# Experts 1 to 7 of a mixture make their first product by Strassen's algorithm

## The chip, the core and the metric

The kernel runs on one core of a Trainium2 chip. Five engines work side by side, each through its own instructions in order: TensorE (PE, matrix products into PSUM), VectorE (DVE), ScalarE (ACT), GpSimd (POOL, no access to PSUM, also issues indirect transfers) and SyncE (SP, issues the other transfers). They wait for each other by semaphores. The metric is the device time of one execution in microseconds, median of several. PSUM has eight banks of 512 float32 values per partition.

## The reference

`setup_inputs` gives q, k, v (4 batches, 8 heads, 768 positions, 64 values) and the weights of a mixture of 8 experts. Local and block-compressed attention makes x, 3072 rows of 512. Then every row goes to its two best experts:

```
logits = x @ w_gate;  noisy = logits + log1p(exp(x @ w_noise)) * noise
top2 = two largest of noisy;  top2_w = softmax over the two
for e in range(8):
    for k in range(2):
        mask = top2[:, k] == e
        h = np.maximum(x[mask] @ w1[e], 0.0)                     # 512 -> 1024
        out[mask] += top2_w[mask, k, None] * (h @ w2[e])         # 1024 -> 512
```

## The kernel before

Attention and gating fill the first 150 us or so; the change doesn't touch them. A table then says which rows each expert has. Space is made for 816 rows (`CAP`) per expert, in seven chunks: six of 128 and one of 48.

Every float32 operand is split into two float16 values, a high part (rounded) and a low part (the rest). A product is three products: high by high, low weight by high, high weight by low. ACT makes a high part by a copy, DVE the low part as operand minus high part.

For each expert:

- `x_gather` (POOL) fetches a chunk's rows of x, high and low side by side, into one of four buffers `xg`; `x_trans` (SP) transposes them by a transfer into `xte`, 8 blocks of 128 partitions (4 high, 4 low) by 816 rows.
- `w_load` (SP) fetches a quarter of a weight matrix, 512 KB, into one of four buffers `stg`; `w_split` makes its high part on ACT and its low part on DVE. Both weight matrices have two sets of buffers, one for odd experts and one for even ones.
- First product: for two halves of the rows (384 and 432 wide) and eight blocks f of 128 of the 1024 columns, `mm1` runs 12 matmuls into a bank `h` (four banks in turn). ACT writes `hth` = relu(h) in float16, DVE writes `htl` = max(h, 0) - hth.
- Second product: for each chunk, three passes of eight matmuls into a bank `pt` (two banks in turn): `hth` by `w2h`, `htl` by `w2h`, `hth` by `w2l`. Then DVE makes `y` = pt x gate + `prev`, where `prev` (three buffers) holds the rows of `out` as earlier experts left them, fetched by POOL; POOL writes y back to those rows.

What prepares expert e + 1 is issued in steps between the pieces of expert e: `ticks` is called after each block of the first product and each chunk of the second, and `next_loads` issues at each call one load and split, or one gather and transpose. So the order of each engine's instructions is the order of the program's text, and an engine that waits for one instruction holds up all that stand behind it in that order.

The last lines of the program, under `tc.If`, serve inputs where an expert has more than 816 rows; with these inputs they don't run.

Of the kernel before, what the change touches and what calls it, by code (L numbers as in the profile page):

```python
# [59 lines left out]
def attn_moe(ctx, tc, qt, kt, vt, wgn, noise, w1, w2, out):  # L60
# [565 lines left out]
    def w_lo(e, i):  # L626
        n, sc = ("w1", W1S) if i < 4 else ("w2", W2S)
        hi, lo = [WT[e][n + x][:, i % 4, :] for x in "hl"]
        nc.vector.scalar_tensor_tensor(lo, SG[e, i], sc, hi, op0=OP.mult, op1=OP.subtract)  # L629

# [112 lines left out]
    def mm2_high(e, c, hook=None, py=None):  # L743
        PY[c] = psum.tile([P, 512], F32, name="pt", bufs=2) if py is None else py
        mm2_pass(e, c, "w2h", HT[0], 0, PY[c])
        if hook:
            hook()
        mm2_pass(e, c, "w2h", HT[1], 1, PY[c])

    def mm2_low(e, c, pv):  # L750
# [4 lines left out]
        gw = (TL[:, e] if c == LAST else tb_of(e, c)).bitcast(F32)[:, 1:2]
        if pv is None:
            nc.vector.tensor_scalar(y, py[:, :d], gw, None, op0=OP.mult)
# [297 lines left out]
    late_k = k
    tick = [0]

    def ticks(e):
        if e == 1 and tick[0] + late_k < 18:
            next_loads(1, tick[0] + late_k)  # L1060
        else:
            next_loads(e + 1, tick[0] - (18 - late_k if e == 1 else 0))
        tick[0] += 1

    for e in range(1, E):
        tick[0] = 0
        pv = []
        for half in range(2):
            for f in range(FC):
                mm1(e, half, f)  # L1070
                ticks(e)
                if tick[0] > 13:
                    pv.append(prev_gather(e, len(pv)))
# [112 lines left out]
```

## Time and profile before

| | |
|---|---|
| median of 3 runs | 702.61 us |
| lowest, highest | 702.22, 704.16 us |
| span of the profiled execution | 701.2 us |
| mean granted clock of TensorE | 0.992 |
| busy in that span: PE, DVE, ACT, POOL | 668.8, 314.2, 236.4, 248.4 us |
| transfers | 125.90 MB, 180 GB/s on average |

The profile is of one execution; its own time outside the span isn't given, and the median lies 1.4 us above its span. In the lines of the profile, L690 is the matmul of the first product, L740 and L737 those of the second (six whole chunks, the last chunk), L700 and L701 the high and low part of h, L612 and L629 those of the weights, L757 and L759 y, L86 POOL's indirect transfers, L604 and L607 the loads of weights, L668 the transposes. L352, L512 and L622 lie in the attention and gating: L352 is a POOL subtraction of two operands, L512 and L622 are DVE instructions with two operands in SBUF. Idle time behind a group is time in which its engine had nothing running, with what ended it.

### The profile page before, as it was taken

Reading aid. Unit: us, or ns where it says so; the run is one execution under the profiler, and the core shown is the slowest. Engines: PE = TensorE matmul, PEld = TensorE weight load, DVE = VectorE, ACT = ScalarE, POOL = GpSimd, SP = SyncE. Lnnn points to the kernel's source line nnn. Section 1 sums busy time; section 2 is a strip of 40 time slices with the busy share of each in tenths; the row PEclk is TensorE's granted clock in tenths of the full one; section 3 lists DMA queues with packets and bytes.
Section 4 is the critical chain, followed back from the end, with each engine's and each line's share of the span. In section 5 each row is a group of like instructions: output and inputs, shape, how many; then the busy total and the mean of one; then the engine's idle time right before and its main releaser. Section 6 shows DMA issues by size and latency. Waiting matters only on the chain.

```text
span 701.2 us, 14039 instructions
## 1 busy us (share of the span) xinstructions
PE 668.8 (95%) x5568; PEld 386.3 (55%) x5568; DVE 314.2 (45%) x663; ACT 236.4 (34%) x538; POOL 248.4 (35%) x435
## 2 busy tenths in 40 slices
PE   7999889889999999999999999999999999999993
PEld 6677667665445544654465456545554555455442
DVE  5758898789443533253134314521442155122110
ACT  2879788842231430142024203400430043012100
POOL 3445344502605305432343234233414441530141
PEclk9999999999999999999999999999999999999997
DMA  9999998867885997494259617921994196320021
GB/s 285 303 281 332 275 318 271 240 178 285 213 195 157 195 218 200 138 264 168 87 124 218 200 68 184 306 67 69 178 231 151 64 211 186 103 61 16 28 80 35
DMA packets 100295, 125.90 MB, mean 180 GB/s; under 512 B 58985, under 2 KB 63857, under 8 KB 100220
## 3 DMA queue, kind: packets, MB, share of 16 engines
q1 hardware_dynamic: 88076, 88.64, 48.3%
q0 software_dynamic: 12144, 36.28, 17.6%
q8 instruction: 46, 0.75, 0.5%
q14 instruction: 29, 0.24, 0.1%
HBM read 87.57 MB, written 26.21 MB: 162 GB/s over the span
## 4 chain that ended last, share of the span: by engine, by line
PE 82%; DVE 7%; ACT 4%; DMA 3%; issue 1%; SPq 0%; POOL 0%; POOLq 0%; DVEq 0%
PE h L690 37%; PE pt L740 35%; PE pt L737 3%; ACT p L304 2%; PE pt L310 2%; DMA hth<-in_vt_dram 1%; PE s L290 1%; DMA q<-in_qt_dram 1%; PE o L323 1%; DVE rh L535 1%; DVE nm L297 1%; ACT pts L313 1%; DMA kb<-in_kt_dram 1%; PE pt L235 1%; DVE kmax L218 1%
## 5 line engine op out<-in xcount | busy, mean ns | idle before, releaser
L690 PE MATMUL h<-xte,w1h 128*128 128x432 f16 (+1 forms) x1024 | 199.4, 336 | 0.6 <-ACT xte L677 0.6
L700 ACT ACTIVATE hth<-h 128x432 f16<-128x432 f32 (+1 forms) x128 | 64.1, 508 | 301.1 <-PE h L690 289.2
L690 PEld LDWEIGHTS <-w1h 128*128 128x128 f16 x1024 | 99.5, 98 | 76.8 <-issue 2.0
L86 POOL DMA_INDIRECT out_dram<-y,tb x48 | 53.2, 1109 | 249.0 <-DVE y L759 219.3
L740 PEld LDWEIGHTS <-hth 128*128 128x128 f16 x768 | 75.0, 98 | 90.0 <-ACT hth L700 0.8
L701 DVE SCALAR_TENSOR_TENSOR htl<-h,hth 128x432 f16<-128x432 f32 (+1 forms) x128 | 73.3, 580 | 94.7 <-ACT hth L700 89.5
L690 PE MATMUL h<-xte,w1l 128*128 128x432 f16 (+1 forms) x512 | 109.3, 336 | 0.0
L759 DVE SCALAR_TENSOR_TENSOR y<-pt,tb,prev 128x512 f32<-128x512 f32 x42 | 31.5, 751 | 162.0 <-PE pt L740 157.6
L86 POOL DMA_INDIRECT xg<-xd,tb x56 | 60.8, 1085 | 92.7 <-DMA xte<-xg 55.5
L740 PE MATMUL pt<-w2h,hth 128*128 128x512 f16 x376 | 89.2, 379 | 0.0
L740 PE MATMUL pt<-w2h,htl 128*128 128x512 f16 x376 | 88.8, 379 | 0.0
L740 PE MATMUL pt<-w2l,hth 128*128 128x512 f16 x376 | 88.7, 379 | 0.0
L690 PEld LDWEIGHTS <-w1l 128*128 128x128 f16 x512 | 50.1, 98 | 38.0
L740 PEld LDWEIGHTS <-htl 128*128 128x128 f16 x384 | 37.6, 98 | 45.2
L304 ACT ACTIVATE p<-s,nm 128x118 f32<-128x118 f32 x192 | 53.3, 376 | 0.8
L629 DVE SCALAR_TENSOR_TENSOR w2l<-stg,w2h 128x1024 f16<-128x1024 f32 x32 | 38.8, 1222 | 26.0 <-ACT w2h L612 21.6
L612 ACT ACTIVATE w2h<-stg 128x1024 f16<-128x1024 f32 x32 | 33.7, 1053 | 49.9 <-DMA stg<-in_w_dram 49.8
L352 POOL TENSOR_TENSOR xr<-x,xr 128x512 f16<-128x512 f32 x22 | 25.4, 1156 | 63.0 <-ACT xr L345 35.2
L86 POOL DMA_INDIRECT prev<-out_dram,tb x42 | 42.6, 1015 | 10.8 <-issue 10.8
L629 DVE SCALAR_TENSOR_TENSOR w1l<-stg,w1h 128x1024 f16<-128x1024 f32 x28 | 34.3, 1225 | 25.7 <-ACT w1h L612 24.9
L612 ACT ACTIVATE w1h<-stg 128x1024 f16<-128x1024 f32 x28 | 29.4, 1051 | 15.0 <-DMA stg<-in_w_dram 14.8
L310 PE MATMUL pt<-ident,p 128*118 128x128 f32 x192 | 29.7, 286 | 1.6 <-ACT p L304 1.6
(166 smaller groups left out, 572.1 us busy)
## 6 DMA issues: line engine op xcount, KB each, us to landing
stg<-in_w_dram SPq DMA_DIRECT2D x64, 512.0 KB
hth<-in_vt_dram SPq DMA_DIRECT2D x8, 780.0 KB
vw<-in_vt_dram SPq DMA_DIRECT2D x32, 195.0 KB
q<-in_qt_dram SPq DMA_DIRECT2D x24, 256.0 KB
xd<-xr SPq DMA_DIRECT2D x24, 256.0 KB
out_dram<-xg SPq DMA_DIRECT2D x8, 768.0 KB
kb<-in_kt_dram SPq DMA_DIRECT2D x6, 768.0 KB
htl<-in_vt_dram SPq DMA_DIRECT2D x16, 195.0 KB
```

What stands on the lines that cost most here:

```text
L86: return nc.gpsimd.indirect_dma_start(**kw)
L304: nc.scalar.activation(PE_[t][:, a, hp, :], SC[t][:, a, hp, :], AF.Exp, bias=NM[t][:, 1, a, hp:hp + 1], scale=0.125)
L310: nc.tensor.transpose(pt[:NK, hp, :], PE_[t][:, a, hp, :], ident)
L352: engine.tensor_tensor(XR[t][:, DM:], X[t], XR[t][:, 0:DM], op=OP.subtract)
L612: nc.scalar.activation(WT[e][n + "h"][:, i % 4, :], SG[e, i], AF.Copy, scale=sc)
L629: nc.vector.scalar_tensor_tensor(lo, SG[e, i], sc, hi, op0=OP.mult, op1=OP.subtract)
L690: nc.tensor.matmul(ph[:, :n], w[wn][:, c, f * P:(f + 1) * P], x[:, xo + c, c0:c1], start=(k == 0), stop=(k == 11), skip_group_check=hook i ...
L700: nc.scalar.activation(hh[:, f, c0:c1], ph, AF.Relu)
L701: nc.vector.scalar_tensor_tensor(hl[:, f, c0:c1], ph, 0.0, hh[:, f, c0:c1], op0=OP.max, op1=OP.subtract)
L737: nc.tensor.matmul(py[64 * r:64 * r + 64, :HD], hx[:, f, c * P:c * P + 64], w[:, f, HD * r:HD * r + HD], start=first, stop=final, skip_gro ...
L740: nc.tensor.matmul(py, hx[:, f, c * P:c * P + P], w[:, f, :], start=first, stop=final, skip_group_check=True)
L759: nc.vector.scalar_tensor_tensor(y, py[:, :d], gw, pv[:, :d], op0=OP.mult, op1=OP.add)
```

## The change

For experts 1 to 7 the first product is cut into 2 by 2 blocks: the 512 values that are summed over into two halves, the 1024 columns into two halves, and the 816 rows into two halves of 408. Seven products of blocks take the place of eight, by the variant of Strassen's algorithm with shared sums:

```
w1 as blocks:  a.l a.r (upper half of the 512)   b.l b.r (lower half)
x as blocks x[half of the 512][half of the rows], low and high part joined
S1 = a.r + b.r     S2 = S1 - a.l      S3 = a.l - a.r     S4 = b.l - S2
T1 = x01 - x00     T3 = x11 - x01     T2 = T3 + x00      T4 = x10 - T2
P1 = a.l x00   P2 = b.l x10   P3 = S4 x11   P4 = b.r T4   P5 = S1 T1   P6 = S2 T2   P7 = S3 T3
u2 = P6 + P1       u3 = P6 + P7 + P1
left columns:  first rows a = P1 + P2     second rows c1 = P5 + P3 + u2
right columns: first and second rows c2 = P4 + u3 | P5 + u3
```

The sums and their places in the code stand in the diff. The sums S are made by POOL (`w1_sums`) and split by ACT and DVE (`w1_pair`); b.r of the loaded weight goes into its place, S4 takes the place of a.r. The differences of x are made by POOL (`t_diff`), the rest of the T by DVE, and split again by ACT (`t_hi`) and DVE (`t_lo`). `mm1_quad` makes the products of one block f of 128 columns in each half of the columns, four times per expert, in the order P1, P6, P5, P7, P4, P2, P3. P1 and P2 gather in a bank `o` of two; P6 and P7 in one bank `h`, P5 and P3 in a second, P4 in a third. P7 is added to the bank of P6, and u2 reads P6 from it in between, so P7 waits for u2.

The second weights have one set of buffers in place of two and are split during the first product of their own expert. Steps are now written into `plan`: 28 in the first product (after each of the seven products), 21 in the second (after the first and second pass and after y). Of a y there are two buffers in place of four. In expert 0, whose matmuls stay as they were, all that prepares expert 1 is issued in 13 steps, among them what was done in expert 1 before.

```diff
     def w_alloc(e):
+        w1_alloc(e)
+        w2_alloc(e)
+
+    def w1_alloc(e, sums=False):
         pool = late[0] if e % 2 else wpool
-        WT[e] = {n: pool.tile([P, 4, 1024], F16, name=f"{n}{e % 2}") for n in ("w1h", "w1l", "w2h", "w2l")}
+        WT[e] = {n: pool.tile([P, 4, 1024], F16, name=f"{n}{e % 2}") for n in ("w1h", "w1l")}
...
+    def w2_alloc(e):
+        for n in ("w2h", "w2l"):
+            WT[e][n] = wpool.tile([P, 4, 1024], F16, name=n)
...
+    def w1_sums(e, k):
+        a, b = SG[e, k], SG[e, k + 2]
+        s = WS_[e, k] = side_pool[0].tile([P, 4, HF], F32, name="ws")
+        nc.gpsimd.tensor_tensor(s[:, 0], a[:, HF:], b[:, HF:], op=OP.add)
+        nc.gpsimd.tensor_tensor(s[:, 2], a[:, :HF], a[:, HF:], op=OP.subtract)
+        nc.gpsimd.tensor_tensor(s[:, 1], s[:, 0], a[:, :HF], op=OP.subtract)
+        nc.gpsimd.tensor_tensor(s[:, 3], b[:, :HF], s[:, 1], op=OP.subtract)
+
+    def w1_pair(e, k, part):
...
+        if part == 0:
+            todo_ = [(hi[:, k, :HF], lo[:, k, :HF], SG[e, k][:, :HF]),
+                     (hi[:, k + 2], lo[:, k + 2], SG[e, k + 2])]
+        else:
+            s = WS_[e, k]
+            todo_ = [(w["sh"][:, :, k], w["sl"][:, :, k], s[:, 0:3]),
+                     (hi[:, k, HF:], lo[:, k, HF:], s[:, 3])]
+        for h, _, x in todo_:
+            nc.scalar.activation(h, x, AF.Copy, scale=W1S)
+        for h, l, x in todo_:
+            nc.vector.scalar_tensor_tensor(l, x, W1S, h, op0=OP.mult, op1=OP.subtract)
...
+    def t_diff(e, j, low):
+        i = (1, 1) if j == 3 else (0, 1)
+        o = (0, 1) if j == 3 else (0, 0)
+        nc.gpsimd.tensor_tensor(tt(e, (j, low)), xb(e, *i, low), xb(e, *o, low), op=OP.subtract)
...
+    def h_split(f, c0, c1, c, hook=None):
+        hh, hl = HT
+        nc.scalar.activation(hh[:, f, c0:c1], c, AF.Relu)
...
+        nc.vector.scalar_tensor_tensor(hl[:, f, c0:c1], c, 0.0, hh[:, f, c0:c1], op0=OP.max, op1=OP.subtract)
+
+    def mm1_quad(e, f, oa, tick):
...
+        a = oa[:, f % 2, :HC]
+        product(a, e, f, 1, True, False)
+        p1 = temp("p1")
+        nc.scalar.activation(p1, a, AF.Copy)
+        tick()
+        b = bank()[:, 0, :HC]
+        product(b, e, f, 6, True, False)
+        u2 = temp("u2")
+        nc.vector.tensor_add(u2, b, p1)
+        tick()
+        d = bank()[:, 0, :HC]
+        product(d, e, f, 5, True, False)
+        tick()
+        product(b, e, f, 7, False, True)
+        u3 = temp("u3")
+        nc.vector.tensor_add(u3, b, p1)
+        c2 = temp("c2", 2 * HC)
+        nc.vector.tensor_add(c2[:, HC:], d, u3)
+        tick()
+        c = bank()[:, 0, :HC]
+        product(c, e, f, 4, True, True)
+        nc.vector.tensor_add(c2[:, :HC], c, u3)
+        h_split(f + FC // 2, 0, CAP, c2)
+        tick()
+        product(a, e, f, 2, False, True)
+        h_split(f, 0, HC, a)
+        tick()
+        product(d, e, f, 3, False, True)
+        c1 = temp("c1")
+        nc.vector.tensor_add(c1, d, u2)
+        h_split(f, HC, CAP, c1)
+        tick()
...
+    def t_steps(e, where, ks):
+        for k, fs in zip(ks, (
+            ((t_alloc, ()), (t_diff, (3, 0)), (t_diff, (3, 1))),
+            ((w1_pair, (0, 0)),),
+            ((w1_pair, (0, 1)),),
+            ((t_diff, (1, 0)), (t_join, (3,)), (t_two, (0,))),
+            ((t_two, (1,)), (t_hi, (2,)), (t_hi, (3,)), (t_diff, (1, 1))),
+            ((t_lo, (2,)), (t_lo, (3,))),
...
+    put(0, 4, w1_sums, 1, 0)
+    put(0, 6, w1_sums, 1, 1)
+    t_steps(1, 0, (8, 5, 6, 9, 10, 10, 7, 8, 11, 11, 12, 12))
...
+    for e in range(1, E):
+        put(e, 0, w2_alloc, e)
+        for i in range(4):
+            put(e, 7 * i + 3, w_split, e, 4 + i)
...
+        put(e, 18, w1_sums, n, 0)
+        put(e, 29, w1_sums, n, 1)
+        t_steps(n, e, range(28, 40))
```

Where this puts instructions, in three places. First, DVE in the first product of an expert. Before, each block f had its low part, with a split of a weight after every second:

```order
L701 SCALAR_TENSOR_TENSOR htl<-h,hth 128x384 [waits Activation_49] x4
L629 SCALAR_TENSOR_TENSOR w1l_3838<-stg,w1h_3837 128x1024 [waits DMAHW6_49,Activation_49]
L701 SCALAR_TENSOR_TENSOR htl<-h,hth 128x384 [waits Activation_49] x2
L629 SCALAR_TENSOR_TENSOR w1l_3838<-stg,w1h_3837 128x1024 [waits DMAHW7_49,Activation_49]
L701 SCALAR_TENSOR_TENSOR htl<-h,hth 128x432 [waits Activation_49] x2
```

Now one pass of `mm1_quad`, from u2 to the next u2 (o is the bank of P1 and P2, h those of the others):

```order
L829 TENSOR_TENSOR u2_4471<-h_4464,p1_4456 128x408 [waits PE_49,Activation_49]
L836 TENSOR_TENSOR u3_4492<-h_4464,p1_4456 128x408 [waits PE_49]
L838 TENSOR_TENSOR c2_4494<-h_4479,u3_4492 128x408 [waits DVE_49]
L643 SCALAR_TENSOR_TENSOR w2l_4459<-stg_4294,w2h_4458 128x1024 [waits DMAHW1_49,Activation_49]
L842 TENSOR_TENSOR c2_4494<-h_4498,u3_4492 128x408 [waits PE_49]
L815 SCALAR_TENSOR_TENSOR htl_88<-c2_4494,hth_87 128x816 [waits Activation_49]
L815 SCALAR_TENSOR_TENSOR htl_88<-o_4449,hth_87 128x408 [waits Activation_49]
L850 TENSOR_TENSOR c1_4529<-h_4479,u2_4471 128x408 [waits PE_49]
L815 SCALAR_TENSOR_TENSOR htl_88<-c1_4529,hth_87 128x408 [waits Activation_49]
L829 TENSOR_TENSOR u2_4553<-h_4546,p1_4539 128x408 [waits PE_49,Activation_49]
```

Nine instructions stand where a quarter of the first product had four low parts and one or two splits, and four of the nine wait for ACT.

Second, DVE in the second product of an expert, where before only y and what was left of the second weights stood (ws: POOL's sums, sl: their low parts, tt: the T in float32, tx: the T split):

```order
L668 SCALAR_TENSOR_TENSOR w1l1_4461<-stg_4521,w1h1_4460 128x512 [waits DMAHW7_49,Activation_49]
L668 SCALAR_TENSOR_TENSOR w1l1_4461<-stg_4597,w1h1_4460 128x1024 [waits DMAHW2_49,Activation_49]
L908 SCALAR_TENSOR_TENSOR y_4812<-pt_4773,tb_175,prev1_2972 128x512 [waits DMASW1_49,DMASW0_49,PE_49]
L668 SCALAR_TENSOR_TENSOR sl1_4463<-ws_4665,sh1_4462 128x3x512 [waits Activation_49]
L668 SCALAR_TENSOR_TENSOR w1l1_4461<-ws_4665,w1h1_4460 128x512 [waits Activation_49]
L686 TENSOR_TENSOR tt_4783<-tt_4783,tt_4785 128x816 [waits Pool_49]
L690 TENSOR_TENSOR tt_4838<-tt_4783,xte_4473 128x816 [waits DMAHW5_49,DMAHW1_49,DMAHW6_49,DMAHW0_49,DVE_49]
L692 TENSOR_TENSOR tt_4838<-tt_4838,xte_4473 128x816 [waits DVE_49]
L908 SCALAR_TENSOR_TENSOR y_4861<-pt_4826,tb_175,prev2_2973 128x512 [waits DMASW2_49,PE_49]
L709 TENSOR_TENSOR tx_4782<-tt_4838,tx_4782 128x816 [waits Activation_49]
L709 TENSOR_TENSOR tx_4782<-tt_4783,tx_4782 128x816 [waits Activation_49]
```

Behind these stand four more splits of weights, like the first two and the two of `ws`, and then the third y; so each y stands behind the work for the next expert.

Third, DVE in expert 0, in the last rows of its own first product (htl_88<-h is the low part of one block f; the last row is that of the eighth):

```order
L668 SCALAR_TENSOR_TENSOR sl1_2970<-ws_3509,sh1_2969 128x3x512 [waits Activation_49]
L668 SCALAR_TENSOR_TENSOR w1l1_2968<-ws_3509,w1h1_2967 128x512 [waits Activation_49]
L781 SCALAR_TENSOR_TENSOR htl_88<-h_3567,hth_87 128x432 [waits Activation_49]
L668 SCALAR_TENSOR_TENSOR w1l1_2968<-stg_3431,w1h1_2967 128x512 [waits DMAHW2_49,Activation_49]
L668 SCALAR_TENSOR_TENSOR w1l1_2968<-stg_3433,w1h1_2967 128x1024 [waits DMAHW3_49,Activation_49]
L781 SCALAR_TENSOR_TENSOR htl_88<-h_3586,hth_87 128x432 [waits Activation_49]
L668 SCALAR_TENSOR_TENSOR sl1_2970<-ws_3558,sh1_2969 128x3x512 [waits Activation_49]
L668 SCALAR_TENSOR_TENSOR w1l1_2968<-ws_3558,w1h1_2967 128x512 [waits Activation_49]
L781 SCALAR_TENSOR_TENSOR htl_88<-h_3610,hth_87 128x432 [waits Activation_49]
L686 TENSOR_TENSOR tt_3602<-tt_3602,tt_3604 128x816 [waits Pool_49]
L690 TENSOR_TENSOR tt_3628<-tt_3602,xte_3401 128x816 [waits DMAHW5_49,DMAHW4_49,DMAHW6_49,DMAHW1_49,DVE_49]
L781 SCALAR_TENSOR_TENSOR htl_88<-h_3630,hth_87 128x432 [waits Activation_49]
```

Before, four splits of loaded weights stood between those low parts, none of which waits for POOL; now splits of POOL's sums and two instructions on POOL's differences do.

More of the change, by code (lines that the diff above doesn't have):

```diff
@@ L36 @@
 H0, CAP = 384, 816
+HF, HC = F // 2, CAP // 2
 QN = 3
@@ L74, in attn_moe @@
     keep = attn.enter_context(tc.tile_pool(name="keep", bufs=1))
-    work = ctx.enter_context(tc.tile_pool(name="work", bufs=2, side="right"))
+    works = ExitStack()
+    work = works.enter_context(tc.tile_pool(name="work", bufs=2, side="right"))
+    side_pool = []
     ctx.enter_context(tc.manual_schedule())
@@ L594, in w_alloc @@
     def w_alloc(e):
+        w1_alloc(e)
+        w2_alloc(e)
+    def w1_alloc(e, sums=False):
         pool = late[0] if e % 2 else wpool
-        WT[e] = {n: pool.tile([P, 4, 1024], F16, name=f"{n}{e % 2}") for n in ("w1h", "w1l", "w2h", "w2l")}
+        WT[e] = {n: pool.tile([P, 4, 1024], F16, name=f"{n}{e % 2}") for n in ("w1h", "w1l")}
+        if sums:
+            for n in ("sh", "sl"):
+                WT[e][n] = late[0].tile([P, 3, 2, HF], F16, name=f"{n}{e % 2}")
+    def w2_alloc(e):
+        for n in ("w2h", "w2l"):
+            WT[e][n] = wpool.tile([P, 4, 1024], F16, name=n)
     SG = {}
@@ new lines, in w1_pair @@
+    def w1_pair(e, k, part):
+        w = WT[e]
+        hi, lo = w["w1h"], w["w1l"]
+        if part == 0:
[9 more added lines that the diff above has]
+            nc.vector.scalar_tensor_tensor(l, x, W1S, h, op0=OP.mult, op1=OP.subtract)
@@ new lines, in t_two, with t_four, t_alloc, t_of @@
+    def t_two(e, low):
+        if low == 0:
+            nc.vector.tensor_add(tt(e, 2), TT[e, (3, 0)], xb(e, 0, 0, 0))
+        else:
+            nc.vector.tensor_add(TT[e, 2], TT[e, 2], xb(e, 0, 0, 1))
+    def t_four(e):
+        c = TT[e, 2]
+        nc.vector.tensor_sub(c, xb(e, 1, 0, 0), c)
+        nc.vector.tensor_add(c, c, xb(e, 1, 0, 1))
+    def t_alloc(e):
+        TX[e] = side_pool[0].tile([P, 2, 4, 2, HC], F16, name="tx")
+    def t_of(e, j):
+        return TT[e, (j, 0)] if j in (1, 3) else TT[e, 2]
@@ L705, in mm1, with product @@
         mm1_out(e, half, f)
+    MP = {}
+    def product(o, e, f, p, start, stop):
+        w = WT[e]
+        if p in (1, 2, 4):
+            c, a = {1: (0, 0), 2: (2, 0), 4: (2, HF)}[p]
+            lhs = [w[n][:, c:c + 2, a + f * P:a + f * P + P] for n in ("w1h", "w1l")]
+        elif p == 3:
+            lhs = [w[n][:, 0:2, HF + f * P:HF + f * P + P] for n in ("w1h", "w1l")]
+        else:
+            lhs = [w[n][:, p - 5, :, f * P:f * P + P] for n in ("sh", "sl")]
+        if p <= 3:
+            j, k = {1: (0, 0), 2: (1, 0), 3: (1, 1)}[p]
+            rhs = [xb(e, j, k, low) for low in range(2)]
+        else:
+            rhs = [TX[e][:, low, {4: 4, 5: 1, 6: 2, 7: 3}[p] - 1] for low in range(2)]
+        n = 0
+        for a, b in ((0, 0), (1, 0), (0, 1)):
+            for c in range(2):
+                nc.tensor.matmul(o, lhs[a][:, c], rhs[b][:, c], start=start and n == 0, stop=stop and n == 5,
+                                 skip_group_check=True)
+                n += 1
@@ L1052, in attn_moe, with ticks @@
         mm2(0, c, None)
-        next_loads(1, k)
+        step(0, k)
         k += 1
[L1055 to L1063, printed above, removed]
-    for e in range(1, E):
-        tick[0] = 0
-        pv = []
[L1068 to L1073, printed above, removed]
+    for e in range(1, E):
+        tick = [0]
+        def ticks():
+            step(e, tick[0])
+            tick[0] += 1
+        oa = psum.tile([P, 2, 512], F32, name="o")
+        pv = []
+        for f in range(FC // 2):
+            mm1_quad(e, f, oa, ticks)
+        for c in range(3):
+            pv.append(prev_gather(e, c))
         for c in range(NCH):
-            mm2(e, c, pv[c])
-            ticks(e)
+            mm2(e, c, pv[c], ticks)
             if len(pv) < NCH:
                 pv.append(prev_gather(e, len(pv)))
+    assert not plan, plan
     def over_chunk(e, c):
```

88 lines of the change are left out of this document (67 added, 21 removed).

## The prediction

> **What bounds the kernel now.** I read the page's top first, then the stretches, then the chain of waits, and went from there to single rows. The stretches of 50 us through the experts (columns: stretch, length, then busy us of PE, weight loads, DVE, ACT, POOL, then the granted clock, DMA share and GB/s):
>
> ```profile
> 200.00:250.00 50.00, 49.97 (x303) 27.24 (x302) 21.71 (x29) 15.72 (x26) 17.89 (x30) 1.00 0.79 192
> 250.00:300.00 50.00, 50.00 (x291) 25.97 (x289) 18.03 (x23) 11.72 (x17) 20.25 (x36) 1.00 0.73 178
> 600.00:650.00 50.00, 50.00 (x302) 27.12 (x301) 10.46 (x18) 6.57 (x13) 13.21 (x24) 1.00 0.17 53
> ```
>
> From 200 us on TensorE never rests, at full clock, and DVE works 18 to 22 of 50 us. One expert in the chain of waits (start, length, piece):
>
> ```profile
> 354.56 33.23 PE h L690 x192
> 387.79 31.08 PE pt L740 x144
> 418.87 2.74 PE pt L737 x48
> 421.61 33.23 PE h L690 x192
> ```
>
> An expert takes 67.05 us: 33.23 of first product, 33.82 of second, nothing between. So TensorE is the bound, and fewer products would shorten the program by all they cost, as long as nobody makes PE wait. That is what has to be examined.
>
> **What it removes.** 7 of 8 products at the mean width (408 lies midway between 384 and 432): 33.23 x 7/8 = 29.08 us, 1.04 us for one block product. Removed: 4.15 us an expert, 29.0 us for seven. If PE never waited, the time would be 702.6 - 29.0 = 673.6.
>
> **What it adds inside the first product.** In each of the four row passes DVE now has nine instructions, in the order shown in the section on the change. Their prices come from these rows (mean ns of one behind the comma; of a pair, the time of both):
>
> ```profile
> L701 DVE SCALAR_TENSOR_TENSOR htl<-h,hth 128x432 f16<-128x432 f32 x52 | 31.1, 605 | 34.0 <-ACT hth L700 33.7
> L701 DVE SCALAR_TENSOR_TENSOR htl<-h,hth 128x384 f16<-128x384 f32 x56 | 30.8, 555 | 50.5 <-ACT hth L700 46.3 <-issue 4.2
> L629 DVE SCALAR_TENSOR_TENSOR w1l<-stg,w1h 128x1024 f16<-128x1024 f32 x24 | 29.4, 1224 | 18.1 <-ACT w1h L612 17.5 <-issue 0.7
> L700 ACT ACTIVATE hth<-h 128x432 f16<-128x432 f32 x53 | 27.5, 527 | 51.4 <-PE h L690 49.7 <-issue 1.7
> L612 ACT ACTIVATE w1h<-stg 128x1024 f16<-128x1024 f32 x24 | 25.2, 1051 | 8.9 <-DMA stg<-in_w_dram 8.7
> 385.82 1.23 DVE L629 SCALAR_TENSOR_TENSOR w2l<-stg,w2h 128x1024 f16<-128x1024 f32 x1 [3.39 <-ACT w2h L612]
> 386.96 1.11 DVE L701 SCALAR_TENSOR_TENSOR htl<-h,hth 128x432 f16<-128x432 f32 x2
> L338 DVE TENSOR_TENSOR x<-o,ri 128x512 f32<-128x512 f32 x22 | 15.2, 692 | 2.2
> ```
>
> 48 columns more cost DVE 50 ns, so 408 columns take 0.58 us, 816 take 1.01, 1536 take 1.76. The adds out of PSUM have no row of their own; the nearest, the product of L338 at 512 columns, comes to the same 0.58 when 104 columns are taken off it. A follower that needs nothing of its predecessor starts earlier: 1.14 us after the start of a 1024, 0.50 after a 432; so 0.48 for 408, 0.92 for 816, 0.60 for 512, 1.67 for 1536. ACT: 0.51 for 408, 0.87 for 816 (between 432 and 1024). The delays between engines:
>
> ```profile
> 215.84 1.89 PE L740 MATMUL pt<-w2l,hth 128*128 128x512 f16 x8
> 217.77 0.75 DVE L757 TENSOR_SCALAR y<-pt,tb 128x512 f32<-128x512 f32 x1 [3.30 <-PE pt L740]
> 356.66 0.49 ACT L700 ACTIVATE hth<-h 128x384 f16<-128x384 f32 x1 [34.40 <-PE h L690]
> 357.18 0.56 DVE L701 SCALAR_TENSOR_TENSOR htl<-h,hth 128x384 f16<-128x384 f32 x1 [2.09 <-ACT hth L700]
> 183.59 0.49 ACT L677 ACTIVATE xte<-h 128x384 f16<-128x384 f16 x1 [1.06 <-PE h L676]
> 184.14 0.89 PE L690 MATMUL h<-xte,w1h 128*128 128x432 f16 x4 [0.64 <-ACT xte L677]
> ```
>
> PE to reader 0.20 (eight of these matmuls take 31.08/18 = 1.73, so PE was done at 217.57), ACT to DVE 0.03, ACT to PE 0.06; I take 0.03 from DVE to itself and to ACT, 0.06 to PE. Product 7 goes into the bank that u2 reads, so it waits for u2. From one u2 to the next: u2 0.58 and 0.06, product 7 1.04 and 0.20, u3 0.61, the first half of c2 0.48, the low half of a second weight 1.14, the other half of c2 0.61, ACT's 816 columns 0.90, DVE's 816 0.92, the low part of a 0.48, c1 0.61, ACT 0.54, its low part 0.48: 8.65 us. Seven products take PE 7.27. The first pass is covered, since DVE comes to it idle; the other three wait 1.38 each, 4.1 us. At the end the second product wants the last high part of a, which ACT writes 0.72 after it starts on the 816 columns: another 0.6. Together 4.7 us against 4.15 saved: **+0.6 an expert, 4.2 for seven.** The arithmetic that was removed comes back as waiting for DVE.
>
> [...]
>
> **The shared way into SBUF.** Before, POOL does no arithmetic among the experts. Now it does eight sums of 512 and four differences of 816 per expert. What that does to DVE is seen only in the attention (of L512 and L622: least/median/most ns):
>
> ```profile
> L512 DVE TENSOR_TENSOR wa<-wa,p x6: 149/152/437, 73.3 to 160.5; 128x4 f32<-128x4 f32 x6
> 73.31 0.44 DVE L512 TENSOR_TENSOR wa<-wa,p 128x4 f32<-128x4 f32 x1
> 72.58 1.15 POOL L352 TENSOR_TENSOR xr<-x,xr 128x512 f16<-128x512 f32 x1 [0.90 <-DVE xr L349]
> L622 DVE SCALAR_TENSOR_TENSOR w1l<-stg,w1h x8: 678/684/1331, 62.3 to 115.0; 128x512 f16<-128x512 f32 x8
> 62.30 1.33 DVE L622 SCALAR_TENSOR_TENSOR w1l<-stg,w1h 128x512 f16<-128x512 f32 x1
> 61.93 1.16 POOL L352 TENSOR_TENSOR xr<-x,xr 128x512 f16<-128x512 f32 x1 [0.42 <-POOL kx L113]
> ```
>
> Four columns that need 0.15 us took 0.44 and ended at 73.75, when POOL's instruction ended (73.73). A 684 ns split lasted until 0.54 us after POOL's (63.09). Both DVE instructions read two SBUF operands. I read this as: such a DVE instruction and a POOL sum run one after the other. By these rows a POOL sum costs 1.16, a difference 816/512 of it, 1.8.
>
> In the first product four sums meet DVE's two-operand splits in the third and fourth pass: 0 to 4.6 us, I take 0.7 (most of DVE's time there goes to PSUM operands and waits), **4 us for six experts** (the last one prepares none).
>
> In the second product, counted from its start T: the last u2 began 0.64 and four products, 4.8, before T, and the low part of c1 follows it by 8.17, so DVE comes free at T + 3.9. Up to the y of the third chunk it has, in the printed order, eight weight splits (twice 0.60, 1.14, 1.67 and 0.60: 8.0), five operand instructions (three that follow each other at 1.04, two at 0.92: 5.0) and three y's (2.1 at 0.75 in the row above, less overlap): done at T + 19.0. PE wants that bank again, for the fifth chunk, at T + 0.6 + 4 x 5.18 = T + 21.3. Without POOL nothing waits. With POOL's two differences, four sums and two more differences (3.6 + 4.6 + 3.6) wholly in between, y is done at T + 30.8 and PE waits 9.5; with only the first six, less the y's, which read PSUM and can run beside them, T + 25.1, a wait of 3.8. I take 5.5, nearer the lower since POOL gets in while DVE waits for ACT: **33 for six experts**, ends 0 and 57.
>
> **Expert 0.** It keeps its matmuls, but prepares expert 1, and DVE's low parts of its own h stand behind that work. The last (row 7) stands behind two instructions that wait for POOL's second difference. POOL starts here:
>
> ```profile
> 180.70 1.04 POOL L86 DMA_INDIRECT out_dram<-y,tb  x1 [1.29 <-DVE y L757]
> 187.51 1.01 POOL L86 DMA_INDIRECT xg<-xd,tb  x1 [0.22 <-issue]
> 188.83 1.00 POOL L86 DMA_INDIRECT xg<-xd,tb  x1 [0.23 <-PE h L690]
> 203.75 1.89 PE L740 MATMUL pt<-w2h,htl 128*128 128x512 f16 x8
> ```
>
> Three scatters and seven gathers at 1.32 (188.83 - 187.51), eight sums at 1.16 and two differences at 1.8: 26.1, to 206.8; the second four sums wait 1.3 more for DVE to read the first (one buffer). Then two DVE instructions and the low part: 210.7. PE wants it at the end of the pass that began at 203.75, at 205.3. So at least 5 us; the transposes and weights that POOL needs come by DMA, and in this stretch
>
> ```profile
> 199.25 1.06 ACT L612 ACTIVATE w1h<-stg 128x1024 f16<-128x1024 f32 x1 [5.63 <-DMA stg<-in_w_dram]
> 190.89 0.53 SPq L604 DMA_DIRECT2D stg<-in_w_dram  x1
> ```
>
> a load takes 8.4. SP's queue holds all four loads between the first transposes now. Range 5 to 20, I take **12**: two loads of that length in a row would make it 20, none 5.
>
> Second weights in one buffer: they are written in the first product, after PE has left the old ones, and the last split ends before the second product starts: 0, unless a load is late.
>
> **Sum.** The profiled execution spans 701.2, the median is 1.4 above it: 701.2 + 1.4 + 4.2 + 4 + 33 + 12 = **756**.
>
> **Rivals.** The port does not matter (0.19): DVE and POOL overlap, the terms 4 and 33 vanish, expert 0 keeps 9 to 16: 716 to 723. Two slow rows of many speak for the other reading, but few overlaps are to be seen. Faster (0.09): DVE's chain is shorter than I add. From under 7.27 us a pass nothing waits; then the seven experts give up to 29 and expert 0 takes 5: 679 to 700. The place is the stretch from u2 to the next u2; for it speaks that DVE starts a follower before the predecessor is done. Against it: that overlap is in the sum already, and 8.65 would have to lose 16% although least and median of a group differ by 1%. Late loads (0.12): a second-weight split stands inside DVE's chain, so a load that has not landed stops a pass; two such waits of 2 us an expert add 28: 784. Forecast 0.6.
>
> The range goes from the port rival to the upper ends, 716 to 783. A difference under 0.3%, 2.1 us, can't be told from none: faster 0.08, same 0.03, slower 0.89.
>
> **What would show it.** PE idle before product 7 of passes 2 to 4, about 1.4 us, released by u2; before the fourth and fifth chunk's first pass, released by y; some 10 us around 200 us, released by htl. POOL sums and DVE splits stretched where they overlap, DVE busy over 32 of 50 us. The last expert, without POOL sums, should last 67.6. If experts 1 to 6 last under 67, the chain is wrong; if all last 67.6, the port is.

## The result: 13.5% slower

The changed kernel takes 797.6 us (median of four, 796.79 to 800.92), the kernel before beside it 702.93 us: a ratio of 1.135, 95% interval 1.133 to 1.138. Forecast were 756 us, with a range from 716 to 783. The sign was right; 42 us were not in the sum, and the time lies outside the range.

The profiled execution spans 795.0 us. On its page PE is no longer busy throughout, POOL and DVE work far more, and the granted clock has gaps:

```profile
PE 669.7 (84%) x5400; PEld 374.4 (47%) x5400; DVE 518.9 (65%) x873; ACT 289.3 (36%) x594; POOL 421.2 (53%) x519
PE   7988889799597798889878987898789977997894
PEclk9999999999889999989999999899999999999998
```

The stretches of experts 1 to 7 (columns as in the prediction: stretch, length, busy us of PE, weight loads, DVE, ACT, POOL, granted clock, DMA share, GB/s):

```profile
237.80:317.60 79.80, 67.08 (x363) 33.86 (x362) 53.61 (x61) 23.26 (x32) 49.43 (x54) 0.96 0.53 133
317.60:398.20 80.60, 68.45 (x363) 34.27 (x362) 51.89 (x61) 23.26 (x32) 48.69 (x54) 0.94 0.51 133
398.20:474.80 76.60, 65.58 (x361) 33.34 (x362) 52.97 (x61) 23.26 (x32) 49.34 (x54) 0.98 0.52 140
...
711.50:784.00 72.50, 65.23 (x362) 33.38 (x360) 28.79 (x43) 13.12 (x20) 15.75 (x28) 0.98 0.14 44
```

Before, an expert took 67.05. Now experts 1 to 6 take 76.5 to 80.6 and the last one, which prepares nothing, 72.5. PE is busy 65 to 68 us in them where all products together need 63; the surplus is matmuls at a lower granted clock (0.94 to 0.98 in these rows), the rest is waiting. Over all seven (length, busy PE, clock, DMA share, GB/s):

```profile
237.80:784.00 546.20, 468.29 (x2522) 0.96 0.46 123
```

So PE is idle for 77.9 us there. Whom it waits for stands in the waits by releaser (us in total, times, longest):

```profile
PE o L806 <- DVE htl L815: 53.3, 21, 4.1
PE pt L887 <- DVE y L908: 19.1, 8, 3.1
PE pt L887 <- ACT hth L780: 6.6, 1, 6.6
PE pt L887 <- ACT hth L812: 5.5, 7, 1.7
PE pt L887 <- DVE htl L781: 4.4, 2, 3.1
```

The first row is the surprise. It isn't product 7 behind u2, it is a product that writes `o`: product 1. The timeline of one pass: the first matmuls of product 1 in two passes on PE, and DVE between them (the bracket names the wait and its releaser):

```profile
407.81 0.51 PE L806 MATMUL o<-xte,w1h 128*128 128x408 f16 x2 [2.26 <-DVE htl L815]
417.48 0.51 PE L806 MATMUL o<-xte,w1h 128*128 128x408 f16 x2 [2.26 <-DVE htl L815]
```

```profile
412.15 0.58 DVE L836 TENSOR_TENSOR u<-h,p 128x408 f32<-128x408 f32 x1 [1.42 <-PE h L806]
413.27 1.22 DVE L643 SCALAR_TENSOR_TENSOR w2l<-stg,w2h 128x1024 f16<-128x1024 f32 x1
414.40 0.58 DVE L842 TENSOR_TENSOR c<-h,u 128x408 f32<-128x408 f32 x1
415.92 1.01 DVE L815 SCALAR_TENSOR_TENSOR htl<-c,hth 128x816 f16<-128x816 f32 x1 [0.95 <-ACT hth L812]
416.85 0.58 DVE L815 SCALAR_TENSOR_TENSOR htl<-o,hth 128x408 f16<-128x408 f32 x1
```

Product 1 of each later pass stands 2.26 us or more (4.1 at most), until DVE has written the low part of a (htl<-o, 416.85 + 0.58 = 417.43). a lies in one half of `o`, the next product 1 goes into the other half, but both are one tile, and the wait is for the tile. So the next pass can't begin until the chain of this one is through: product 1, 6, 5 and 7 (4.15), the way to u3 (0.2), u3, the first half of c2, the low half of a second weight, the other half of c2, ACT's relu, and DVE's two low parts. A pass lasts 417.48 - 407.81 = 9.67 us, where PE needs 7.27. The row of its group:

```profile
L806 PE MATMUL o<-xte,w1h 128*128 128x408 f16 x224 | 60.8, 355 | 53.3 <-DVE htl L815 53.3
```

One of these matmuls takes 355 ns on average, where the median is 336. A later run, in which these waits were filled with work and the time fell by 17 us, shows that they slow what follows them.

### The profile page after: what moved, and what is told of

Its sections match the earlier page's. It is cut to its first block, busy times and chain, and to the rows that moved or that the text cites. A ratio compares the mean times of both kernels' runs of the same rounds, so it can differ in the third digit from the quotient of the medians.

```text
span 795.0 us, 14005 instructions
## 1 busy us (share of the span) xinstructions
PE 669.7 (84%) x5400; PEld 374.4 (47%) x5400; DVE 518.9 (65%) x873; ACT 289.3 (36%) x594; POOL 421.2 (53%) x519
## 4 chain that ended last, share of the span: by engine, by line
PE 38%; DVE 26%; ACT 9%; issue 9%; DMA 8%; POOL 7%; SPq 1%; POOLq 0%; DVEq 0%; ACTq 0%
PE pt L887 13%; PE h L806 12%; DVE htl L815 5%; PE o L806 5%; DVE w2l L643 4%; ACT hth L812 4%; PE pt L884 3%; DVE u L836 2%; ACT p L307 2%; DVE w1l L668 2%; DVE c L842 1%; DMA out_dram<-xg 1%; DMA xte<-xg 1%; DVE y L908 1%; DMA hth<-in_vt_dram 1%
## 5 line engine op out<-in xcount | busy, mean ns | idle before, releaser
L887 PE MATMUL pt<-w2h,hth 128*128 128x512 f16 x376 | 94.9, 394 | 31.3 <-DVE y L908 19.1
L812 ACT ACTIVATE hth<-c 128x816 f16<-128x816 f32 (+1 forms) x56 | 39.9, 713 | 189.2 <-DVE c L842 119.1
L806 PE MATMUL o<-xte,w1h 128*128 128x408 f16 x224 | 60.8, 355 | 53.3 <-DVE htl L815 53.3
L806 PEld LDWEIGHTS <-w1h 128*128 128x128 f16 x448 | 43.9, 99 | 92.1 <-issue 62.2
L806 PE MATMUL h<-tx,sh 128*128 128x408 f16 x336 | 83.3, 359 | 0.0
L815 DVE SCALAR_TENSOR_TENSOR htl<-c,hth 128x816 f16<-128x816 f32 (+1 forms) x56 | 46.9, 838 | 43.7 <-ACT hth L812 43.7
L682 POOL TENSOR_TENSOR tt<-xte 128x816 f32<-128x816 f16 x28 | 60.4, 2177 | 27.3 <-DMA xte<-xg 17.0
L650 POOL TENSOR_TENSOR ws<-stg 128x512 f32<-128x512 f32 x14 | 22.2, 1583 | 96.3 <-DVE w1l L668 49.6
L706 ACT ACTIVATE tx<-tt 128x816 f16<-128x816 f32 x28 | 24.0, 879 | 122.6 <-DVE tt L692 52.3
L806 PEld LDWEIGHTS <-sh 128*128 128x128 f16 x336 | 35.2, 105 | 31.0 <-issue 9.5
L806 PE MATMUL h<-tx,sl 128*128 128x408 f16 x168 | 46.6, 362 | 0.0
```

Source lines behind the costliest of these rows:

```text
L682: nc.gpsimd.tensor_tensor(tt(e, (j, low)), xb(e, *i, low), xb(e, *o, low), op=OP.subtract)
L706: nc.scalar.activation(TX[e][:, 0, j - 1], t_of(e, j), AF.Copy)
L806: nc.tensor.matmul(o, lhs[a][:, c], rhs[b][:, c], start=start and n == 0, stop=stop and n == 5, skip_group_check=True)
L812: nc.scalar.activation(hh[:, f, c0:c1], c, AF.Relu)
L815: nc.vector.scalar_tensor_tensor(hl[:, f, c0:c1], c, 0.0, hh[:, f, c0:c1], op0=OP.max, op1=OP.subtract)
L887: nc.tensor.matmul(py, hx[:, f, c * P:c * P + P], w[:, f, :], start=first, stop=final, skip_group_check=True)
```

## The experiments

The rows of the experiments are those of their own kernels, whose line numbers differ by a few.

### Product 1 out of the shared tile

```diff
-        a = oa[:, f % 2, :HC]
+        b, a, d = [bank()[:, 0, :HC] for _ in range(3)]
...
-        c = bank()[:, 0, :HC]
+        c = oa[:, f % 2, :HC]
```

> The sum of a (products 1 and 2) moves to a bank of its own and product 4 takes the half of the two-bank tile, so that product 1 of the next pass no longer waits for VectorE's low part of a. Theory (the wait at product 1 is the shared tile's, and behind it the chain from one u2 to the next limits, 8.65 us): the wait of 2.26 to 2.7 us at product 1 goes, some 1.4 us come back at product 7, the pitch of a pass falls from 9.67 to 8.65 us, expert 7 from 72.5 to 68 to 69.5 us, and the time by 7 x 3 x 1.02 = 21 us and what the clock gives back, to 760 to 777. Rival (VectorE's own work or its order sets 9.67 us whatever the bank): the pitch stays at 9.6 to 9.7, expert 7 over 72, the time within 4 us of 797.6.

769.5 us, ratio 1.091 (1.086 to 1.096): as the theory had it; expert 7 lasts 68.0 us. A group of PE, and two starts of product 7 that follow each other:

```profile
L806 PE MATMUL h<-tx,sh 128*128 128x408 f16 x336 | 83.7, 338 | 32.5 <-DVE u L828 20.6 <-DVE htl L815 11.9
```

```profile
326.43 0.50 PE L806 MATMUL h<-tx,sh 128*128 128x408 f16 x2 [0.98 <-DVE u L828]
335.16 0.51 PE L806 MATMUL h<-tx,sh 128*128 128x408 f16 x2 [0.98 <-DVE u L828]
```

The wait at product 1 is gone, and the one that I had forecast comes up in its place: PE before product 7, released by u2 (in the last pass, in experts 1 to 6, also one of 1.0 to 1.9 us before product 6, released by htl). The pitch is 8.73 us; the prediction's chain from u2 to u2 was 8.65. The chain was right, it stood behind a longer one.

### The split of the second weights, two products earlier

```diff
-            put(e, 7 * i + 3, w_split, e, 4 + i)
+            put(e, 7 * i + 1, w_split, e, 4 + i)
```

> The split of the second weights is put two products earlier, behind u2, where VectorE stood idle for 1.42 us; the shared tile stays. Theory (the wait at product 1 is the end of a serial chain of products 1, 6, 5, 7 and then VectorE's and ScalarE's steps to the low part of a, in which the split's 1.14 us stand): the pitch falls from 9.67 to about 8.53 us, the wait at product 1 from 2.3 to 1.1 to 1.5 us, the time by 7 x 3 x 1.14 = 24 us, to 765 to 777. Rival (VectorE's sum of work, or contention, sets the pitch): pitch 9.5 to 9.7, the time within 5 us of 797.6.

754.9 us, ratio 1.070 (1.064 to 1.075). The pitch came as worked out, 8.53 us:

```profile
398.56 0.51 PE L806 MATMUL o<-xte,w1h 128*128 128x408 f16 x2 [1.12 <-DVE htl L815]
407.09 0.51 PE L806 MATMUL o<-xte,w1h 128*128 128x408 f16 x2 [1.13 <-DVE htl L815]
```

So the wait at product 1 is the end of that serial chain: 1.14 us out of it are 1.14 us off the pass, though the work is only moved. By the ratios the time fell by 0.066 of 703, 46 us, where 24 were expected; it lies below the range. The traced execution took 763.7 us, 9 more than the median. In it PE's idle time in experts 1 to 7 falls from 77.9 to 54.0 us, 24, as worked out, and its busy time, for the same matmuls, from 468.3 to 455.2 us: 13, the clock (0.98 in place of 0.96; what a lower clock costs is the subject of a later run). The other 9 are not in this trace.

### Both edits

> Both edits together: product 4 in the shared tile's place and the split of the second weights behind u2. Theory (the two waits were the shared tile's and, under it, the chain on VectorE, and without them TensorE's own 7.27 us are left): the waits at products 1 and 7 are both under 0.3 us, the pitch of a pass is 7.3 to 7.6 us, and the time is 797.6 less 7 x 3 x 2.1 to 2.4 us less some of the clock's loss, 730 to 750. Rival (VectorE's work of a pass in its fixed order is the next bound): a wait of 0.5 to 1.2 us comes back at product 7 or 6, the pitch is 7.8 to 8.6 us, the time 750 or more, no better than the second weights' move alone.

745.9 us, ratio 1.062 (1.054 to 1.070): the two waits together, with the clock they cost, are 0.073 of 703, 52 us. The time is in the theory's range; the pitch, 7.80 us as the mean of an expert's four passes, is at the lower end of the rival's. Most of the wait is gone; 0.2 us remain before product 7 in the second pass and 0.3 to 1.6 in the last two, released by u2. PE's waits for y, 19.1 us in the changed kernel, are 24.6 here.

### GpSimd's arithmetic almost without time

```diff
-        nc.gpsimd.tensor_tensor(s[:, 0], a[:, HF:], b[:, HF:], op=OP.add)
+        nc.gpsimd.tensor_tensor(s[:, 0, :4], a[:, HF:HF + 4], b[:, HF:HF + 4], op=OP.add)
```

and so on for the other three sums and the differences. The rest of each sum is left out; their buffers are fixed ones here, filled with zeros once.

> GpSimd's sums of first weights and differences of tokens are cut to 4 columns of 512 and 2 by 2 of 2 by 408: the same instructions in the same places, with almost no time of their own; the output is no longer the reference's. Theory (GpSimd's arithmetic keeps VectorE from its two-operand work and this is what experts 1 to 6 have beyond expert 7): experts 1 to 6 fall from 76.5 to 80.6 to 71.5 to 74 us each, expert 7 stays at 72.5, expert 0's stall shrinks by 2 to 8 us, the time falls by 30 to 45 us, to 753 to 768. Rival (the port costs nothing, the excess is VectorE's and ScalarE's added work and the late gathers and loads): experts 1 to 6 stay above 75.5 us and the time falls by less than 10 us.

753.0 us, ratio 1.069 (1.062 to 1.077): 46 us less. Groups of PE, two experts, and all seven together:

```profile
L888 PE MATMUL pt<-w2h,hth 128*128 128x512 f16 x376 | 91.4, 382 | 14.4 <-ACT hth L781 11.0 <-ACT hth L813 3.4
L807 PE MATMUL o<-xte,w1h 128*128 128x408 f16 x224 | 60.2, 352 | 47.6 <-DVE htl L816 47.6
```

```profile
309.70:380.50 70.80, 63.54 (x362) 1.00 0.55 151
380.50:453.00 72.50, 65.24 (x362) 0.98 0.55 147
```

```profile
235.50:739.50 504.00, 453.03 (x2520) 0.98 0.48 133
```

All waits for y, 19.1 us in the changed kernel, are gone: they were the price of POOL's arithmetic, not of the two buffers of y. Experts 1 to 6 fall to 70.8 to 72.5 us, the last one stays. The regular wait at product 1, 2.26 us, is untouched, so the two causes are separate; the row falls by 5.7 us, which lay on top of it. PE's idle time falls from 77.9 to 51.0 us, 27, and its busy time by 15, the clock.

That DVE's instructions were stretched, and not merely late for POOL's results, is seen in the changed kernel before such a wait (y at the fifth chunk, 3.08 us, ending at 459.83). DVE goes from one instruction to the next there, and the same split takes 0.69 us at one place and 2.21 at another, beside POOL's differences:

```profile
443.98 0.69 DVE L668 SCALAR_TENSOR_TENSOR w1l<-ws,w1h 128x512 f16<-128x512 f32 x1
456.91 2.21 DVE L668 SCALAR_TENSOR_TENSOR w1l<-ws,w1h 128x512 f16<-128x512 f32 x1
```

With thin POOL work expert 1 still begins at 235.5 (237.8 in the changed kernel): POOL's arithmetic is not what stalls expert 0 for most of that time. POOL stands 10.60 us there before a gather, until a transpose has freed the buffer, and ACT then waits for the sums that come behind it.

### The disputed cost by itself

> Only a probe: groups of 8 VectorE operations of 408 columns (two operands in SBUF; one in PSUM and one in SBUF; one in SBUF; one in PSUM), each alone and beside five GpSimd operations of 816 columns (two operands, one operand, a fill); the output is zeros. Theory (an operation of VectorE with two SBUF operands and one of GpSimd exclude each other for a whole instruction): VectorE's 8 take 8 x 0.44 alone, and single ones grow to 1.2 to 2.6 us beside GpSimd's two-operand ones; those with an operand in PSUM stay at 0.57 to 0.60 us, and a fill disturbs nothing. Rival (a bandwidth is shared): all kinds with an SBUF operand stretch by one like factor of 1.3 to 2 and none waits for a whole operation.

The timeline of DVE's groups of eight, for two SBUF operands, one PSUM and one SBUF operand, and one SBUF operand; first alone, then beside POOL's two-operand work:

```profile
5.39 4.89 DVE L51 SCALAR_TENSOR_TENSOR d<-a,hh 128x408 f16<-128x408 f32 x8
10.26 4.89 DVE L53 TENSOR_TENSOR e<-acc,b 128x408 f32<-128x408 f32 x8
15.13 3.21 DVE L54 TENSOR_SCALAR e<-b 128x408 f32<-128x408 f32 x8
...
23.18 12.81 DVE L51 SCALAR_TENSOR_TENSOR d<-a,hh 128x408 f16<-128x408 f32 x8
23.88 11.05 POOL L46 TENSOR_TENSOR g<-a,b 128x816 f32<-128x816 f32 x5
35.97 4.89 DVE L53 TENSOR_TENSOR e<-acc,b 128x408 f32<-128x408 f32 x8
46.57 11.11 DVE L54 TENSOR_SCALAR e<-b 128x408 f32<-128x408 f32 x8
47.06 9.99 POOL L46 TENSOR_TENSOR g<-a,b 128x816 f32<-128x816 f32 x5
...
92.38 4.89 DVE L51 SCALAR_TENSOR_TENSOR d<-a,hh 128x408 f16<-128x408 f32 x8
102.40 6.04 DVE L54 TENSOR_SCALAR e<-b 128x408 f32<-128x408 f32 x8
```

With two SBUF operands 4.89 us become 12.81, with one PSUM operand 4.89 stay 4.89. Single instructions of the first kind (least, median and most ns):

```profile
L51 DVE SCALAR_TENSOR_TENSOR d<-a,hh x32: 572/582/2166, 5.4 to 96.7; 128x408 f16<-128x408 f32 x32
```

The longest lasts 1.6 us more than alone, and one of POOL's takes 2.0 beside DVE's one-operand work (9.99 for five). So the reading of two rows in the prediction holds nearly: the one waits for most of a POOL instruction, the other runs beside it (4.89). It isn't all of one: 4.89 and 9.99 us one after the other would be 14.9, and both were through in 12.81. The rival, a shared bandwidth, would have stretched every kind with an SBUF operand; the one whose other operand lies in PSUM isn't stretched. Two of my guesses fell. One SBUF operand in float32 is hit as well (3.21 to 11.11), and by a mere fill too (last row, 6.04), where two operands beside a fill keep their 4.89. And alone an instruction with two SBUF operands takes 0.61; the 0.44 was an estimate of mine that no run shows.

### The clock by itself: work in the wait

```diff
+        if f:
+            fill = psum.tile([P, 512], F32, name="pt", bufs=2)
+            for _ in range(2):
+                product(fill[:, :HC], e, f, 1, True, True)
         product(a, e, f, 1, True, False)
```

> The changed kernel with 12 more matmuls ahead of product 1 of passes 2 to 4, about 2.06 us of TensorE work in the wait of 2.26 us, into a bank that nobody reads; nothing else moves. Theory (the idle time of the waits makes the granted clock fall to a half, and this is a cost of its own beside the waits): the pitch of an undisturbed pass stays at 9.67 us, the half-clock stretches in the experts' first products go, the granted clock rises from 0.957 to over 0.97, and the time falls by 8 to 22 us, to 775 to 790. Rival (the clock falls for another reason, or slow stretches are hidden in the waits): the time stays within 3 us of 797.6, or rises.

784.7 us, ratio 1.111 (1.105 to 1.118): 0.024 of 703, 17 us less (13 by the medians), by doing 2.06 us of useless work in each wait. In the traces experts 1 to 7 last 529.9 us in place of 546.2. The granted clock is 0.973, that of experts 1 to 7 0.99 in place of 0.96. The pitch of an undisturbed pass is still 9.67 us, so the waits weren't shortened, and this is what they cost beyond their length.

How it comes about is seen best in the run with thin POOL work, in four stretches of 3.4 us around one wait of 2.26 us at product 1 (length, busy PE and matmuls, weight loads, DVE, ACT, POOL, clock):

```profile
402.85:406.25 3.40, 3.40 (x22) 1.91 (x21) 2.01 (x3) 0.00 (x0) 2.52 (x8) 1.00 0.42 94
406.25:409.67 3.42, 1.16 (x7) 0.59 (x6) 2.47 (x5) 1.28 (x2) 2.98 (x5) 0.99 0.57 184
409.67:413.08 3.41, 3.41 (x11) 1.52 (x10) 0.88 (x2) 1.80 (x3) 0.72 (x3) 0.51 0.82 230
413.08:416.50 3.42, 3.42 (x22) 1.96 (x20) 1.50 (x3) 0.20 (x1) 0.00 (x0) 1.00 0.01 4
```

A stretch with 1.16 us of work is followed by one at half clock (0.51): 11 matmuls in place of 22, 1.7 us lost. In that run every second expert is 1.7 us longer (70.8, 72.5), with the same waits at product 1 in all of them, 2.26 to 2.29 us: the length of a wait alone doesn't decide it, and what does was not shown.

### Expert 0: sums ahead of gathers

```diff
-    put(0, 4, w1_sums, 1, 0)
-    put(0, 6, w1_sums, 1, 1)
+    put(0, 3, w1_sums, 1, 0)
+    put(0, 3, w1_sums, 1, 1)
```

> The changed kernel with expert 1's two groups of weight sums put ahead of the last three gathers in GpSimd's queue; nothing else moves. Theory (expert 0's stall of some 10 us at its second product is GpSimd's queue: the sums of the second half stand behind gathers that wait for buffers, ScalarE's conversion waits for them, and behind it expert 0's relu): the wait for ScalarE's hth at 211.70 falls from 6.64 to under 4 us, expert 1 begins 3 to 8 us earlier than 237.8 and the time falls by 3 to 8 us, to 790 to 795. Rival (the gathers put back cost expert 1 its tokens' transposes, or VectorE is the one that is late): the start of expert 1 and the time stay within 2 us or rise.

796.6 us, ratio 1.135 (1.128 to 1.142): no gain, the rival; expert 1 begins at 239.3, 1.5 us later than in the changed kernel. PE's waits in expert 0, and what DVE's low part stood behind:

```profile
206.12 1.03 PE L887 MATMUL pt<-w2h,hth 128*128 128x512 f16 x2 [3.71 <-ACT hth L780]
221.65 0.61 PE L887 MATMUL pt<-w2h,htl 128*128 128x512 f16 x1 [11.64 <-DVE htl L781]
```

```profile
214.09 5.07 POOL L682 TENSOR_TENSOR tt<-xte 128x816 f32<-128x816 f16 x3 [5.06 <-DMA xte<-xg]
217.51 2.52 DVE L686 TENSOR_TENSOR tt<-tt 128x816 f32<-128x816 f32 x1 [9.47 <-POOL tt L682]
220.99 0.60 DVE L781 SCALAR_TENSOR_TENSOR htl<-h,hth 128x432 f16<-128x432 f32 x1
```

The first wait shrank as I expected (6.64 to 3.71), and the next one grew from 3.10 to 11.64: the gathers, now later, make the transposes late, these POOL's differences, these DVE's join, and behind the join stands the last low part of expert 0's own h. Expert 0 waits for a chain of the preparation of expert 1 that begins with the gathers and their transposes; this other order of POOL's work only moved the wait.

### A version without these causes

Both first edits; all sums and differences on DVE, one instruction at a time over the steps of the second product (three of them in DVE's gap before the low part of c2); expert 1 with its eight products as before, so that expert 0 prepares what it used to.

```diff
-        nc.gpsimd.tensor_tensor(s[:, 0], a[:, HF:], b[:, HF:], op=OP.add)
+        nc.vector.tensor_tensor(s[:, i], x, y, op=op)
...
-        h_split(f + FC // 2, 0, CAP, c2)
+        h_split(f + FC // 2, 0, CAP, c2, lambda: step(e, ("x", f)))
...
+        if e == 1:
+            for u in range(2 * FC):
+                mm1(e, u // FC, u % FC)
```

> The two edits of the run with both, and besides: GpSimd's sums and differences are done by VectorE, one operation at a time over the ticks of the second product and in the gap between c2's relu and its low part; expert 1 keeps the eight-product code, so that expert 0 prepares what it prepared before. Theory (with the waits gone and no GpSimd arithmetic beside VectorE, the saving of 4.15 us an expert is left): passes of 7.3 to 7.6 us, experts 2 to 7 of 63 to 65.5 us each against 67.05 before, expert 0 as before, so 702.6 less 6 x 1.5 to 4 us: 678 to 695. Rival (VectorE, with about 57 to 60 us of work in each expert, becomes the bound, and the second product waits for y or for the preparation): experts 2 to 7 take 67 to 72 us and the time is 703 to 735.

695.1 us, ratio 0.986 (0.982 to 0.990): 1.4% faster than before, 0.1 us above the range that I expected. Experts 2 to 7 take about 65.4 us, the pitch (here and below the mean of an expert's four passes) is still 7.86. What PE waited for was DVE's order: a sum that stood in pass 2 and waited for its load, and u2 behind the low part of c1. Both moved:

```diff
+        for g in c1_low:
+            g()
...
-        put(at, ("x", 1), w1_sum, e, 0, 2)
-        put(at, ("x", 2), w1_sum, e, 0, 0)
+        put(at, ("x", 2), w1_sum, e, 0, 2)
+        put(at, ("x", 3), w1_sum, e, 0, 0)
```

> The repaired kernel with two moves in VectorE's queue: the first sum of weights no longer stands in pass 2, where it waited for its load (8.0 us in 5 waits), but a pass later, and the low part of c1 comes after the next pass's u2 instead of ahead of it. Theory (what is left of the passes' waits, 0.2 to 1.0 us at product 7 and 2.06 us once, is VectorE's order and that late load): product 7 waits under 0.15 us, the pitch falls from 7.86 to 7.3 to 7.5 us, experts 2 to 7 from 65.4 to 63.3 to 64.3 us, the time from 695.1 by 6 to 13 us, to 682 to 689. Rival (VectorE's sum of work in a pass, now with the sums, is the bound): the pitch stays at 7.7 to 7.9 us and the time within 3 us of 695.1.

688.8 us, ratio 0.979 (0.975 to 0.982). The time is in the range; the pitch, 7.63, and the experts, 64.45 us, aren't: 0.35 us stay before product 7 in the last two passes. DVE and ACT at one of these waits, which ends at 369.04:

```profile
368.40 0.58 DVE L834 TENSOR_TENSOR u<-h,p 128x408 f32<-128x408 f32 x1 [1.01 <-ACT p L830]
```

```profile
367.42 0.54 ACT L859 ACTIVATE hth<-c 128x408 f16<-128x408 f32 x1 [1.66 <-DVE c L857]
367.87 0.49 ACT L830 ACTIVATE p<-h 128x408 f32<-128x408 f32 x1
```

u2 waits for ACT's copy of P1, which stands behind a relu that waited 1.66 us for DVE. (In the order of one pass shown with the change, five of the nine instructions name ACT, not four: u2 is one of them.) So the copy goes first:

```diff
         nc.scalar.activation(p1, a, AF.Copy)
+        for g in c1_high:
+            g()
```

> The kernel before this one with one move in ScalarE's queue: the copy of P1 comes ahead of the last pass's relu of c1 instead of behind it. Theory (the 0.35 us that TensorE still waits at product 7 is u2 waiting for that copy, which stands behind the relu; ScalarE was idle for 1.66 us before the relu): the wait falls under 0.1 us, the pitch of a pass from 7.63 to 7.25 to 7.35 us, experts 2 to 7 from 64.45 to 63.1 to 63.6 us, and the ratio to before from 0.979 to 0.965 to 0.973. Rival (u2 is late for product 6 or for VectorE's c1, and the copy only ends last by little): the pitch stays within 0.1 us of 7.63 and the ratio within 0.004 of 0.979.

680.2 us, ratio 0.966 (0.963 to 0.969), in the expected range. The groups of PE's two products with the highest idle time in expert code before it:

```profile
L903 PE MATMUL pt<-w2h,hth 128*128 128x512 f16 x376 | 89.2, 379 | 1.5 <-ACT hth L784 1.4
L810 PE MATMUL h<-tx,sh 128*128 128x408 f16 x288 | 66.4, 336 | 0.5
```

An expert now lasts 63.16 us (starts at 352.62 and 415.78), its first product 29.24. The arithmetic of seven products was put at 29.08 in the prediction, and 6 x (67.05 - 63.16) = 23.3 us is nearly what the medians show (703.8 to 680.2, 23.6).

## Why the prediction was wrong, step by step

- **The saving, 4.15 us an expert: right.** The last run shows a first product of 29.24 us for 29.08, and an expert shorter by 3.9.
- **The prices of single instructions: right on DVE and ACT, low on POOL.** The adds out of PSUM at 408 columns take 0.57 to 0.58, the low part of 816 columns 1.01, ACT's 816 0.88; forecast were 0.58, 1.01 and 0.87. The chain from u2 to u2, 8.65, is 8.73 where it is the one that limits. A sum on POOL takes 1.25 us at the least and 1.6 on average, for 1.16, a difference 1.72 and 2.18, for 1.8.
- **"Product 7 ... waits for u2 ... the other three wait 1.38 each": the step that failed.** I followed DVE's order from u2 to u2 and took the one wait of PE that the text of the change names. PE's own first wait in a pass, product 1 for the tile `o`, was not looked for. By the same prices its chain is 9.65 us long, a whole microsecond more than the one I worked out, and so it decides. Four passes are 3 x 9.67 + 7.24 = 36.25, and in an undisturbed expert 0.48 more until the second product has its high part, against 33.8 forecast: 2.9 an expert, 20 us.
- **The clock: missing from the sum.** The kernel before never lets PE rest in the experts (469.30 us busy from 220.40 to 689.70) and its granted clock there is 1.00, and I priced a wait at its length. An undisturbed expert at full clock has 63.5 us of busy time (the row of 70.80 us with thin POOL work), seven have 444.8; here they have 468.3: 24 us. The granted clock of 0.96 over 546 us says nearly the same, as an estimate: if it is time at full and at half clock alone, 0.08 of the time is at half, half of it lost, 22 us. Filling the waits at product 1 gives 17 of it back, taking POOL's work off 15; each with the other's waits still there, so the two can't be added. With 4.5 in expert 0 (below) the clock cost 28 us.
- **The shared way into SBUF, 4 + 33 us: right that DVE is held up, size too large.** The probe shows who waits and how long (4.89 us became 12.81); that a shared way is behind it is my reading. Thin POOL work takes 46 us off; 15 of them are clock and 2 belong to expert 0. In PE's waits it is 27 us: 8 in the first product, for 4, and 19.1 for y, for 33. PE waits for y where the sum had it, before the fifth chunk, in two experts again before the sixth; but 2.7 to 3.1 us there, less than the 3.8 of the lower case. This error hid 10 us of the others.
- **Expert 0, 12 us: right in waits, too small by the clock.** PE's three waits there are 6.64 + 1.29 + 3.10 = 11.0, released by hth and htl. Expert 1 begins 17.4 us later than before: these 11.0, 1.3 that lie ahead of the experts, 0.6 for gathered rows, and 4.5 that I put down to the clock (0.81 in this stretch). The cause was wider than "DVE's low parts of its own h stand behind that work": ACT's high part stood behind a conversion of POOL's sums too, POOL behind gathers that waited for transposes, and another order only moved the wait.
- **Second weights in one buffer: 0, as put**, and the rival of late loads did not come: of the 53.3 us at product 1 no row is released by a load. Two buffers of y cost nothing either, once POOL's work was off.

Together: 20 + 28 - 10 - 1 + 2 = 39, where 42 us were missing; 3 stay open. The range ended too early as well: the upper ends that the prediction gives its terms (4.6 an expert or 27.6 for 4, 57 for 33, 20 for 12) would have made 812, not 783, though none of them stands for what was missing. The forecast's test, "the last expert should last 67.6", found it at once: it lasts 72.5 without any POOL arithmetic.

## What to carry to other kernels

When a change gives TensorE new waits, list them from TensorE's own order, each with the tile that it names, and work out the chain behind every one; the longest decides, and the two halves of one tile counted as one here (2.26 us at product 1). The waits of 2.26 us and more between matmuls cost more than their length here: filled with useless work they gave back 17 us, and behind one of them the granted clock was 0.51. Arithmetic that was moved to GpSimd wasn't free while VectorE read only SBUF (in the probe 4.89 us became 12.81, and 3.21 became 11.11): on VectorE itself, put into gaps, the same sums left an expert of the last version at 63.16 us, where its products need 62.9.
